# Queries and keys transposed by DMA instead of on TensorE, in a fused window attention and MoE kernel

## The chip, the cores and the metric

The kernel runs on one core of a Trainium2 chip. The time is device microseconds of that core; a kernel's time is the median of its runs. Ratios are computed as the mean time of one kernel's fast runs over that of the other's of the same rounds, so they are not quite the ratio of the medians quoted. In the profile PE is TensorE (PEld its weight loads), DVE is VectorE, ACT is ScalarE, POOL is GpSimd, and SP is the engine whose queue issues most DMAs. L198 is line 198 of the kernel that the sentence names.

## The reference

```python
# q, k, v: (8 batches, 8 heads, 576 tokens, 64)
scores = 0.125 * q @ k.T                       # per batch and head
scores = where(abs(i - j) <= 32, scores, -1e9) # a window of 65 keys
x      = softmax(scores) @ v                   # (4608 tokens, 512)
h      = x @ w_in                              # 512 -> 2048
out    = leaky_relu(h, 0.01) @ w_out           # 2048 -> 512
```

## The kernel before

Heads are taken in pairs (p and p + 4), so that 2 x 64 dimensions fill the 128 rows of a matmul (`128*128` in the trace). There are 64 attention steps: 8 batches x 2 halves of 288 tokens x 4 pairs. They are interleaved with MoE work, so that PE always has something to do. The parts that matter here:

```python
RUN = S // 96                        # 6 tokens = 1.5 KB per partition and head
def load_qk(b, p, behind=None):      # one DMA for q, one for k
    for into, src, name in ((qf, q, "qf"), (kf, k, "kf")):
        t = fload.tile([96, 2, RUN * D], FP32, name=f"{name}{p}")
        if behind is not None:       # a guard: a one-element DMA that waits for w_in
            nc.sync.dma_start(out=t[0:1, 0, 0:1], in_=behind.bitcast(FP32))
            behind = None
        nc.sync.dma_start(out=t, in_=src[b, p:H:NPAIR].rearrange("a (p c) d -> p a (c d)", c=RUN))
...
def transposes(b, first=False):      # six per tensor and pair, one group per yield
    ...
        for c in range(RUN):
            nc.tensor.transpose(tp[:, c], src[:, p, c].rearrange("p a d -> p (a d)"), ident[0:96, 0:96])
        tok = tp.rearrange("p c i -> p i c")        # back to token order, on ACT
        if which == "q":
            nc.scalar.activation(out=qT[b][:, p].rearrange("p (i c) -> p i c", c=RUN), in_=tok, func=AF.Copy)
        else:
            kT = attn.tile([128, S], BF16, name="kT")
            nc.scalar.activation(out=kT_v, in_=tok, func=AF.Copy)
            for a in range(2):                      # the key copies, into a block diagonal
                r = slice(64 * a, 64 * a + 64)
                nc.vector.tensor_copy(out=kbd[b % 2][r, p, :, r], in_=kT[r].rearrange("p (n j) -> p n j", j=64))
        yield
...
def weighted(i):                     # s: row sums, x: weighted values
    nc.tensor.matmul(s, ones_bd, pr[:, 0:HALF], start=True, stop=False, ...)
    nc.tensor.matmul(s[:, ...], ones_bd, pr[:, HALF:NCOL], start=False, stop=True, ...)
    ...                              # five matmuls into x
    nc.vector.reciprocal(r, s)
    nc.vector.tensor_mul(xT[:, p, t0:t0 + HALF], x, r)
```

The row sums `s` and the values `x` have one PSUM bank each, the matmul results `mm` three, the transposes one. In the steady part a batch's transposes come one group of six per step.

The softmax here doesn't subtract the row's maximum and nothing guards it: scores larger than these inputs give would overflow.

Of the kernel before, what the change touches and what calls it, by code (L numbers as in the profile page):

```python
# [16 lines left out]
def kernel(  # L17
# [11 lines left out]

    nc = tc.nc  # L30
# [23 lines left out]
    mmps = ctx.enter_context(tc.tile_pool(name="mmps", bufs=3, space=PS))  # L54
    scps = ctx.enter_context(tc.tile_pool(name="scps", bufs=1, space=PS))
    xps = ctx.enter_context(tc.tile_pool(name="xps", bufs=1, space=PS))
    tps = ctx.enter_context(tc.tile_pool(name="tps", bufs=1, space=PS))


    qf, kf, vf = {}, {}, {}  # L60
    RUN = S // 96

    def load_qk(b, p, behind=None):


        for into, src, name in ((qf, q, "qf"), (kf, k, "kf")):
            t = fload.tile([96, 2, RUN * D], FP32, name=f"{name}{p}")
            if behind is not None:
                nc.sync.dma_start(out=t[0:1, 0, 0:1], in_=behind.bitcast(FP32))
                behind = None  # L70
            nc.sync.dma_start(  # L71
                out=t, in_=src[b, p:H:NPAIR].rearrange("a (p c) d -> p a (c d)", c=RUN),
            )
            into[b, p] = t
# [33 lines left out]

    qb = const.tile([96, NPAIR, RUN, 2, D], BF16)
    kb = const.tile([96, NPAIR, RUN, 2, D], BF16)  # L110

# [5 lines left out]
    def clear(t, p):  # L117
# [12 lines left out]
        [(0, 0, 96), (2, 96, 128), (4, 224, 64), (1, 32, 128), (3, 160, 128)],  # L130
        [(4, 288, 64), (6, 352, 128), (8, 480, 96), (5, 288, 128), (7, 416, 128)],
    ]
    ODD = [32, 0]

    win = const.tile([128, 3, 128], BF16)
    nc.gpsimd.memset(win, 1.0)
    for lo in (0, 64):
# [3 lines left out]
            base=0, channel_multiplier=-1, pattern=[[0, 3], [1, 128]],  # L141
# [3 lines left out]
            base=2 * W, channel_multiplier=1, pattern=[[0, 3], [-1, 128]],  # L145
        )
    win_f = win.rearrange("p n c -> p (n c)")
    mask = [const.tile([128, NCOL], BF16, name=f"mask{i}") for i in range(2)]

    def make_masks():  # L150
        for hf in range(2):
            lo = W * (hf + 1)
            nc.gpsimd.tensor_copy(out=mask[hf][:, 0:HALF], in_=win_f[:, lo:lo + HALF])
            nc.gpsimd.tensor_copy(out=mask[hf][:, HALF:NCOL], in_=win_f[:, 0:NCOL - HALF])
# [8 lines left out]
    def cast_qk(b, p, q_eng=None):  # L163
        for eng, src, dst in ((q_eng or nc.gpsimd, qf, qb), (nc.gpsimd, kf, kb)):
            eng.tensor_copy(  # L165
                out=dst[:, p], in_=src[b, p].rearrange("p a (c d) -> p c a d", d=D),
            )
# [9 lines left out]
    def transposes(b, first=False):  # L177

        qT[b] = attn.tile([128, NPAIR, S], BF16, name="qT")
        for p in range(NPAIR):  # L180
            for which, src in (("q", qb), ("k", kb)):
                if first:
                    tp = mmps.tile([128, RUN, 96], BF16, name="tp0", tag="mm")
                else:
                    tp = tps.tile([128, RUN, 96], BF16, name="tp")
                for c in range(RUN):
                    nc.tensor.transpose(  # L187
                        tp[:, c],
                        src[:, p, c].rearrange("p a d -> p (a d)"),
                        ident[0:96, 0:96],  # L190
                    )

                tok = tp.rearrange("p c i -> p i c")
                if which == "q":
                    nc.scalar.activation(  # L195
                        out=qT[b][:, p].rearrange("p (i c) -> p i c", c=RUN), in_=tok, func=AF.Copy,
                    )
                else:  # L198
                    kT = attn.tile([128, S], BF16, name="kT")
                    kT_v = kT.rearrange("p (i c) -> p i c", c=RUN)  # L200
                    nc.scalar.activation(out=kT_v, in_=tok, func=AF.Copy)  # L201
# [272 lines left out]
```

## Time and profile before

The time before is 355.9 us in four runs, and 356.2 to 356.4 in later rounds.

| from the page of before | busy, share of 353.9 us | to be read as |
|---|---|---|
| PE | 324.3 us, 92% | the bound from 28 us on |
| DVE | 211.8 us, 60% | second; one reciprocal of 1.95 us per step |
| ACT | 183.4 us, 52% | has room |
| POOL | 178.7 us, 51% | has room |
| hardware DMA queue | 42.7% of 16 engines | share 0.9 to 1.3 until 53 us and 1.1 to 1.2 from 71 to 106, between and after these 0.1 to 0.6 |

A share of the whole span hides the stages, so the prediction starts from the table of windows.

### The profile page before, as it was taken

Reading aid. Unit: us, or ns where it says so; the run is one execution under the profiler, and the core shown is the slowest. Engines: PE = TensorE matmul, PEld = TensorE weight load, DVE = VectorE, ACT = ScalarE, POOL = GpSimd, SP = SyncE. Lnnn points to the kernel's source line nnn. Section 1 sums busy time; section 2 is a strip of 40 time slices with the busy share of each in tenths; the row PEclk is TensorE's granted clock in tenths of the full one; section 3 lists DMA queues with packets and bytes.
Section 4 is the critical chain, followed back from the end, with each engine's and each line's share of the span. In section 5 each row is a group of like instructions: output and inputs, shape, how many; then the busy total and the mean of one; then the engine's idle time right before and its main releaser. Section 6 shows DMA issues by size and latency. Waiting matters only on the chain.

```text
span 353.9 us, 6635 instructions
## 1 busy us (share of the span) xinstructions
PE 324.3 (92%) x2600; PEld 208.2 (59%) x2624; DVE 211.8 (60%) x242; ACT 183.4 (52%) x363; POOL 178.7 (51%) x213
## 2 busy tenths in 40 slices
PE   2658998999989898999999898999999999999995
PEld 1437864584957655656656555656656656555472
DVE  5588647757686877645653778554676676630101
ACT  5765862292845637518527527716528517326060
POOL 7797676578765766524543568533655423200000
PEclk9999999999999999999999999999999999999999
DMA  8999986599995274342453265340010010020101
GB/s 187 214 205 236 269 162 182 144 201 235 209 255 146 58 222 133 69 126 88 140 162 70 63 177 165 88 124 33 0 61 30 2 61 31 5 86 0 61 31 59
DMA packets 60707, 42.37 MB, mean 120 GB/s; under 512 B 39684, under 2 KB 56068, under 8 KB 60676
## 3 DMA queue, kind: packets, MB, share of 16 engines
q1 hardware_dynamic: 56388, 37.76, 42.7%
q0 software_dynamic: 4288, 4.20, 7.2%
q8 instruction: 20, 0.33, 0.4%
q14 instruction: 11, 0.09, 0.1%
HBM read 36.70 MB, written 9.44 MB: 130 GB/s over the span
## 4 chain that ended last, share of the span: by engine, by line
PE 77%; DMA 7%; DVE 6%; POOL 4%; SPq 2%; issue 2%; ACT 1%; DVEq 0%; POOLq 0%; ACTq 0%
PE mm L273 33%; PE mm L264 31%; DMA kf<-in_k_dram 7%; DVE r L252 5%; PE x L246 3%; PE tp L187 3%; PE ps L220 3%; PE s L238 2%; PE s L239 2%; SPq L71 1%; POOL vbd L175 1%; POOL vbd L400 1%; SPq L82 1%; DVE xT L254 1%; POOL pr L230 1%
## 5 line engine op out<-in xcount | busy, mean ns | idle before, releaser
L252 DVE RECIPROCAL r<-s 128x288 f32<-128x288 f32 x64 | 125.1, 1954 | 38.5 <-PE s L239 38.2
L230 POOL TENSOR_TENSOR pr<-e,mask 128x544 bf16<-128x544 bf16 x64 | 77.7, 1213 | 115.0 <-ACT e L226 114.7
L264 PE MATMUL mm<-xT,w_in_bf 128*128 128x384 bf16 (+1 forms) x896 | 132.7, 304 | 0.9 <-ACT kT L201 0.8
L268 ACT ACTIVATE gT<-mm 128x384 bf16<-128x384 f32 (+1 forms) x224 | 99.0, 445 | 63.0 <-PE mm L264 58.6
L273 PE MATMUL mm<-w_out_bf,gT 128*128 128x512 bf16 x552 | 126.8, 379 | 1.3
L264 PEld LDWEIGHTS <-w_in_bf 128*128 128x128 bf16 x896 | 86.6, 98 | 38.0 <-issue 1.3
L273 PEld LDWEIGHTS <-gT 128*128 128x128 bf16 x576 | 54.9, 98 | 61.1
L226 ACT ACTIVATE e<-ps 128x544 bf16<-128x544 f32 x64 | 39.8, 622 | 77.6 <-PE ps L220 77.6
L280 DVE COPY o_sb<-mm 128x512 f32<-128x512 f32 x36 | 24.9, 691 | 66.8 <-PE mm L273 66.8
L204 DVE COPY kbd<-kT 64x576 bf16<-64x576 bf16 x64 | 28.4, 444 | 18.2 <-ACT kT L201 17.6
L175 POOL CAST vbd<-vf 64x576 bf16<-64x576 f32 x58 | 38.3, 661 | 1.9
L254 DVE TENSOR_TENSOR xT<-x,r 128x288 bf16<-128x288 f32 x64 | 29.3, 458 | 7.0 <-PE mm L264 0.5
L165 POOL CAST kb<-kf 96x768 bf16<-96x768 f32 x32 | 26.6, 834 | 9.5 <-DMA kf<-in_k_dram 9.5
L246 PE MATMUL x<-pr,vbd 128*128 128x128 bf16 (+2 forms) x320 | 26.9, 217 | 2.0 <-POOL vbd L175 1.0
L220 PE MATMUL ps<-qT,kbd 128*128 128x128 bf16 (+2 forms) x320 | 27.3, 219 | 0.3
L238 PE MATMUL s<-pr,ones_bd 128*128 128x288 bf16 x64 | 19.0, 297 | 8.7 <-DVE r L252 7.0
L220 PEld LDWEIGHTS <-kbd 128*128 128x128 bf16 x320 | 21.1, 102 | 8.1 <-issue 0.6
L195 ACT ACTIVATE qT<-tp 128x576 bf16<-128x576 bf16 x32 | 20.8, 649 | 9.6 <-PE tp L187 9.0
L246 PEld LDWEIGHTS <-vbd 128*128 128x128 bf16 x320 | 21.4, 101 | 7.1 <-issue 2.8
L201 ACT ACTIVATE kT<-tp 128x576 bf16<-128x576 bf16 x32 | 20.8, 650 | 8.9 <-PE tp L187 7.9
L187 PE MATMUL tp<-ident,qb 96*128 96x96 bf16 x192 | 14.4, 214 | 8.5 <-DVE qb L165 6.7
L165 POOL CAST qb<-qf 96x768 bf16<-96x768 f32 x24 | 19.7, 820 | 0.0
(31 smaller groups left out, 107.7 us busy)
## 6 DMA issues: line engine op xcount, KB each, us to landing
qf<-in_q_dram SPq DMA_DIRECT2D x32, 288.0 KB, 3.5
kf<-in_k_dram SPq DMA_DIRECT2D x32, 288.0 KB, 3.9
vf<-in_v_dram SPq DMA_DIRECT2D x64, 144.0 KB, 3.4
out_dram<-o_sb SPq DMA_DIRECT2D x36, 256.0 KB, 2.2
w_in_bf<-in_moe_w_in_dram POOLq DMA_DIRECT2D x8, 256.0 KB, 6.4
w_out_bf<-in_moe_w_out_dram POOLq DMA_DIRECT2D x4, 512.0 KB, 13.5
qf<-w_in_bf SPq DMA_DIRECT2D x1, 0.0 KB
vf<-w_out_bf SPq DMA_DIRECT2D x1, 0.0 KB
```

What stands on the lines that cost most here:

```text
L165: eng.tensor_copy(out=dst[:, p], in_=src[b, p].rearrange("p a (c d) -> p c a d", d=D),)
L175: nc.gpsimd.tensor_copy(out=vbd[b % 2][r, p, :, r], in_=vf[b, p][r])
L204: nc.vector.tensor_copy(out=kbd[b % 2][r, p, :, r], in_=kT[r].rearrange("p (n j) -> p n j", j=64),)
L220: nc.tensor.matmul(ps[:, c0:c0 + n], kbd[b % 2][:, p, blk], qT[b][:, p, q0:q0 + n], start=True, stop=True,)
L226: nc.scalar.activation(out=e, in_=ps[:, 512 - HALF:512 - HALF + NCOL], func=AF.Exp, scale=scale,)
L230: nc.gpsimd.tensor_mul(pr, e, mask[hf])
L246: nc.tensor.matmul(x[:, a:a + n], vbd[b % 2][:, p, blk, :], pr[:, c0:c0 + n], start=(n_ == 0), stop=(n_ == len(WIN[hf]) - 1), skip_group_c ...
L252: nc.vector.reciprocal(r, s)
L254: nc.vector.tensor_mul(xT[:, p, t0:t0 + HALF], x, r)
L264: nc.tensor.matmul(h[:, 0:n], w_in_bf[:, c, ts(f, 128)], xT[:, c, ds(t0, n)], start=(c == 0), stop=(c == DMC - 1),)
L268: nc.scalar.activation(out=gT[t0][:, f, 0:n], in_=h[:, 0:n], func=AF.Prelu, alpha=0.01)
L273: nc.tensor.matmul(o, gT[t0][:, f, ts(j, 128)], w_out_bf[:, f, :], start=(f == 0), stop=(f == FFC - 1),)
```

## The change

The intent: take 288 transposes and the ACT copies behind them off the engines, and let the DMA engines, at a share of 0.1 to 0.6 after 106 us, do them. The DMA transposes of the diff leave the columns in the order of the tile they read (so the code is written). So the loads change to runs of four tokens (1 KB) over 48 partitions, queries keep the permuted order through scores, mask and row sums until the last product restores it, and keys are put back in order by the key copy.

```diff
+    qkf = [fload.tile([112, 2, NM, RUN * D], FP32, name=f"qkf{p}") for p in range(NPAIR)]   # RUN = 4, NM = 3
     def load_qk(b, p, behind=None):
-        for into, src, name in ((qf, q, "qf"), (kf, k, "kf")): ...      # one DMA each, 96 partitions
+        for r0, src in ((0, q), (key_row(b), k)):                       # two DMAs each, 48 partitions
             if behind is not None:
                 nc.sync.dma_start(out=rows[0:1, 0, 0, 0:1], in_=behind.bitcast(FP32))
-                behind = None
+            for a in range(2):
+                nc.sync.dma_start(out=rows[:, a],
+                    in_=src[b, NPAIR * a + p].rearrange("(m i c) d -> i m (c d)", i=NR, c=RUN))
...
+    def place_keys(b, p):                                               # the key copies
+            nc.vector.tensor_copy(
+                out=kbd[b % 2][r, p, :, r].rearrange("p n (i c) -> p n i c", c=RUN),
+                in_=t[r].rearrange("p (c n i) -> p n i c", c=RUN, n=NB))
+    def transpose_pe(b, p): ...                                         # batches 0 and 1
+    def transpose_dma(b, p):                                            # batches 2 to 7
+        for r0, t in ((0, qT[b][:, p]), (key_row(b), kT[b, p])):
+            nc.sync.dma_start_transpose(out=t.rearrange("p (g i) -> p g i", i=NR),
+                in_=qkb[r0:r0 + NR, p].rearrange("p c m a d -> p (c m a d)"))
...
+    for b in range(2, B):
+        for p in range(NPAIR):
+            i = 8 * (b - 1) + p + (3 if b == 2 else 0)
+            plan(i + 3, place_keys, b, p)
+            plan(i + 1, transpose_dma, b, p)
+            plan(i, cast_qk, b, p)
+            ...                                                         # and the next loads
```

Cut from it: the masks in the new order, the row sums in five matmuls with the windows of `x` instead of two, one cast for q and k together (halved between DVE and POOL in batches 0 and 1), and a fourth matmul bank in place of the transpose bank.

More of the change, by code (lines that the diff above doesn't have):

```diff
@@ L53, with key_row @@
     PS = bass.MemoryType.PSUM
-    mmps = ctx.enter_context(tc.tile_pool(name="mmps", bufs=3, space=PS))
+    mmps = ctx.enter_context(tc.tile_pool(name="mmps", bufs=4, space=PS))
     scps = ctx.enter_context(tc.tile_pool(name="scps", bufs=1, space=PS))
     xps = ctx.enter_context(tc.tile_pool(name="xps", bufs=1, space=PS))
-    tps = ctx.enter_context(tc.tile_pool(name="tps", bufs=1, space=PS))
-    qf, kf, vf = {}, {}, {}
-    RUN = S // 96
+    vf = {}
+    RUN = 4
+    NI = S // RUN
+    NR = 48
+    NM = NI // NR
+    qkf = [fload.tile([112, 2, NM, RUN * D], FP32, name=f"qkf{p}") for p in range(NPAIR)]
+    def key_row(b):
+        return NR if b < 2 else 64
     def load_qk(b, p, behind=None):
-        for into, src, name in ((qf, q, "qf"), (kf, k, "kf")):
-            t = fload.tile([96, 2, RUN * D], FP32, name=f"{name}{p}")
+        for r0, src in ((0, q), (key_row(b), k)):
+            rows = qkf[p][r0:r0 + NR]
             if behind is not None:
-                nc.sync.dma_start(out=t[0:1, 0, 0:1], in_=behind.bitcast(FP32))
-                behind = None
-            nc.sync.dma_start(
-                out=t, in_=src[b, p:H:NPAIR].rearrange("a (p c) d -> p a (c d)", c=RUN),
-            )
-            into[b, p] = t
+                nc.sync.dma_start(out=rows[0:1, 0, 0, 0:1], in_=behind.bitcast(FP32))
+            for a in range(2):
+                nc.sync.dma_start(
+                    out=rows[:, a],
+                    in_=src[b, NPAIR * a + p].rearrange("(m i c) d -> i m (c d)", i=NR, c=RUN),
+                )
     def load_v(b, p, behind=None):
@@ L106 @@
     nc.vector.memset(ones_bd[64:128, 64:128], 1.0)
-    qb = const.tile([96, NPAIR, RUN, 2, D], BF16)
-    kb = const.tile([96, NPAIR, RUN, 2, D], BF16)
+    qkb = const.tile([112, NPAIR, RUN, NM, 2, D], BF16)
     kbd = [const.tile([128, NPAIR, NB, 128], BF16, name=f"kbd{i}") for i in range(2)]
@@ L129 @@
     WIN = [
-        [(0, 0, 96), (2, 96, 128), (4, 224, 64), (1, 32, 128), (3, 160, 128)],
-        [(4, 288, 64), (6, 352, 128), (8, 480, 96), (5, 288, 128), (7, 416, 128)],
-    ]
-    ODD = [32, 0]
-    win = const.tile([128, 3, 128], BF16)
+        [(0, 0, 24), (2, 24, 32), (4, 56, 16), (1, 8, 32), (3, 40, 32)],
+        [(4, 72, 16), (6, 88, 32), (8, 120, 24), (5, 72, 32), (7, 104, 32)],
+    ]
+    win = const.tile([128, RUN, 32], BF16)
     nc.gpsimd.memset(win, 1.0)
@@ L140 @@
             out=w, in_=w, compare_op=ALU.is_ge, fill=0.0,
-            base=0, channel_multiplier=-1, pattern=[[0, 3], [1, 128]],
+            base=0, channel_multiplier=-1, pattern=[[1, RUN], [RUN, 32]],
         )
@@ L144, with make_mask @@
             out=w, in_=w, compare_op=ALU.is_ge, fill=0.0,
-            base=2 * W, channel_multiplier=1, pattern=[[0, 3], [-1, 128]],
+            base=2 * W, channel_multiplier=1, pattern=[[-1, RUN], [-RUN, 32]],
         )
-    win_f = win.rearrange("p n c -> p (n c)")
     mask = [const.tile([128, NCOL], BF16, name=f"mask{i}") for i in range(2)]
-    def make_masks():
-        for hf in range(2):
-            lo = W * (hf + 1)
-            nc.gpsimd.tensor_copy(out=mask[hf][:, 0:HALF], in_=win_f[:, lo:lo + HALF])
-            nc.gpsimd.tensor_copy(out=mask[hf][:, HALF:NCOL], in_=win_f[:, 0:NCOL - HALF])
+    def make_mask(hf):
+        c0 = 0
+        for blk, q0, n in WIN[hf]:
+            lo = q0 - 16 * blk + 8
+            nc.gpsimd.tensor_copy(
+                out=mask[hf][:, c0:c0 + RUN * n].rearrange("p (c i) -> p c i", c=RUN),
+                in_=win[:, :, lo:lo + n],
+            )
+            c0 += RUN * n
     xT = const.tile([128, NPAIR, NTOK], BF16)
@@ L161, with cast_qk @@
     qT = {}
-    def cast_qk(b, p, q_eng=None):
-        for eng, src, dst in ((q_eng or nc.gpsimd, qf, qb), (nc.gpsimd, kf, kb)):
-            eng.tensor_copy(
-                out=dst[:, p], in_=src[b, p].rearrange("p a (c d) -> p c a d", d=D),
-            )
+    def cast_qk(b, p):
+        rows = slice(0, key_row(b) + NR)
+        src = qkf[p][rows].rearrange("p a m (c d) -> p c m a d", d=D)
+        parts = ((nc.vector, 0, 2), (nc.gpsimd, 2, 4)) if b < 2 else ((nc.gpsimd, 0, 4),)
+        for eng, c0, c1 in parts:
+            eng.tensor_copy(out=qkb[rows, p, c0:c1], in_=src[:, c0:c1])
     def cast_v(b, p, on_act=False):
@@ L175, in cast_v @@
                 nc.gpsimd.tensor_copy(out=vbd[b % 2][r, p, :, r], in_=vf[b, p][r])
-    def transposes(b, first=False):
-        qT[b] = attn.tile([128, NPAIR, S], BF16, name="qT")
-        for p in range(NPAIR):
-            for which, src in (("q", qb), ("k", kb)):
-                if first:
-                    tp = mmps.tile([128, RUN, 96], BF16, name="tp0", tag="mm")
-                else:
-                    tp = tps.tile([128, RUN, 96], BF16, name="tp")
-                for c in range(RUN):
-                    nc.tensor.transpose(
-                        tp[:, c],
-                        src[:, p, c].rearrange("p a d -> p (a d)"),
-                        ident[0:96, 0:96],
-                    )
-                tok = tp.rearrange("p c i -> p i c")
-                if which == "q":
-                    nc.scalar.activation(
-                        out=qT[b][:, p].rearrange("p (i c) -> p i c", c=RUN), in_=tok, func=AF.Copy,
-                    )
-                else:
-                    kT = attn.tile([128, S], BF16, name="kT")
-                    kT_v = kT.rearrange("p (i c) -> p i c", c=RUN)
-                    nc.scalar.activation(out=kT_v, in_=tok, func=AF.Copy)
-                    for a in range(2):
-                        r = slice(64 * a, 64 * a + 64)
-                        nc.vector.tensor_copy(
-                            out=kbd[b % 2][r, p, :, r],
-                            in_=kT[r].rearrange("p (n j) -> p n j", j=64),
-                        )
-                yield
@@ new lines, with new_T @@
+    kT = {}
+    def new_T(b, p):
+        if p == 0:
+            qT[b] = attn.tile([128, NPAIR, S], BF16, name="qT")
+        kT[b, p] = attn.tile([128, S], BF16, name="kT", bufs=3)
+    def place_keys(b, p):
+        t = kT.pop((b, p))
+        for a in range(2):
+            r = slice(64 * a, 64 * a + 64)
+            nc.vector.tensor_copy(
+                out=kbd[b % 2][r, p, :, r].rearrange("p n (i c) -> p n i c", c=RUN),
+                in_=t[r].rearrange("p (c n i) -> p n i c", c=RUN, n=NB),
+            )
@@ new lines, in transpose_pe @@
+    def transpose_pe(b, p):
+        new_T(b, p)
+        for h in range(2):
+            tp = mmps.tile([128, 2 * NM, 2, NR], BF16, name="tp", tag="mm")
+            for g in range(2 * NM):
+                nc.tensor.transpose(
+                    tp[:, g].rearrange("p w i -> p (w i)"),
+                    qkb[0:2 * NR, p, 2 * h + g // NM, g % NM].rearrange("p a d -> p (a d)"),
+                    ident[0:2 * NR, 0:2 * NR],
+                )
+            half = slice(h * S // 2, (h + 1) * S // 2)
+            for w, t in enumerate((qT[b][:, p], kT[b, p])):
+                nc.scalar.activation(
+                    out=t[:, half].rearrange("p (g i) -> p g i", i=NR),
+                    in_=tp[:, :, w], func=AF.Copy,
+                )
+        place_keys(b, p)
@@ L210 @@
+    def transpose_dma(b, p):
+        new_T(b, p)
+        for r0, t in ((0, qT[b][:, p]), (key_row(b), kT[b, p])):
+            nc.sync.dma_start_transpose(
+                out=t.rearrange("p (g i) -> p g i", i=NR),
+                in_=qkb[r0:r0 + NR, p].rearrange("p c m a d -> p (c m a d)"),
+            )
     probs = {}
@@ L218, in score @@
         c0 = 512 - HALF
+        qv = qT[b][:, p].rearrange("p (c i) -> p c i", c=RUN)
         for blk, q0, n in WIN[hf]:
             nc.tensor.matmul(
-                ps[:, c0:c0 + n], kbd[b % 2][:, p, blk],
-                qT[b][:, p, q0:q0 + n], start=True, stop=True,
+                ps[:, c0:c0 + RUN * n].rearrange("p (c i) -> p c i", c=RUN),
+                kbd[b % 2][:, p, blk], qv[:, :, q0:q0 + n], start=True, stop=True,
             )
-            c0 += n
+            c0 += RUN * n
         e = attn.tile([128, NCOL], BF16, name="e")
@@ L235, in weighted @@
         pr = probs.pop(i)
-        x = xps.tile([128, HALF], FP32, name="x")
-        s = xps.tile([128, HALF], FP32, name="s")
-        nc.tensor.matmul(s, ones_bd, pr[:, 0:HALF], start=True, stop=False, skip_group_check=True)
-        nc.tensor.matmul(
-            s[:, ODD[hf]:ODD[hf] + NCOL - HALF], ones_bd, pr[:, HALF:NCOL],
-            start=False, stop=True, skip_group_check=True,
-        )
-        c0 = 0
-        for n_, (blk, q0, n) in enumerate(WIN[hf]):
-            a = q0 - HALF * hf
-            nc.tensor.matmul(
-                x[:, a:a + n], vbd[b % 2][:, p, blk, :], pr[:, c0:c0 + n],
-                start=(n_ == 0), stop=(n_ == len(WIN[hf]) - 1), skip_group_check=True,
-            )
-            c0 += n
-        r = attn.tile([128, HALF], FP32, name="r")
-        nc.vector.reciprocal(r, s)
-        t0 = b * S + hf * HALF
-        nc.vector.tensor_mul(xT[:, p, t0:t0 + HALF], x, r)
+        x = xps.tile([128, RUN, HALF // RUN], FP32, name="x")
+        s = xps.tile([128, RUN, HALF // RUN], FP32, name="s")
+        for out_, weights in ((s, lambda blk: ones_bd), (x, lambda blk: vbd[b % 2][:, p, blk, :])):
+            c0 = 0
+            for n_, (blk, q0, n) in enumerate(WIN[hf]):
+                i0 = q0 - HALF // RUN * hf
+                nc.tensor.matmul(
+                    out_[:, :, i0:i0 + n], weights(blk),
+                    pr[:, c0:c0 + RUN * n].rearrange("p (c i) -> p c i", c=RUN),
+                    start=(n_ == 0), stop=(n_ == len(WIN[hf]) - 1), skip_group_check=True,
+                )
+                c0 += RUN * n
+        r = attn.tile([128, HALF // RUN, RUN], FP32, name="r")
+        nc.vector.reciprocal(r, s.rearrange("p c i -> p i c"))
+        t0 = b * S + hf * HALF
+        nc.vector.tensor_mul(
+            xT[:, p, t0:t0 + HALF].rearrange("p (i c) -> p i c", c=RUN),
+            x.rearrange("p c i -> p i c"), r,
+        )
     gT = {}
@@ L284, with plan @@
     NC = 2 * NPAIR * B
-    state = {"tp": 8, "done": 0}
-    t_parts = {}
-    PLAN = (
-        ((0, 0, 0, 0, 0, 2, 4, 6), ((), (), (), (), (0,), (1, 2), (3,), ()),
-         ((), (), (), (), (), (), (0,), (1, 2, 3))),
-        ((0, 1, 2, 3, 4, 5, 6, 7), ((0,), (1,), (2,), (3,), (), (), (), ()),
-         ((), (), (), (), (0,), (1,), (2,), (3,))),
-    )
-    def step_transposes(upto):
-        while state["tp"] < min(upto, 8 * B):
-            b = state["tp"] // 8
-            if b not in t_parts:
-                t_parts[b] = transposes(b)
-            next(t_parts[b])
-            state["tp"] += 1
+    state = {"done": 0}
+    todo = {}
+    def plan(i, f, *args):
+        todo.setdefault(i, []).append((f, args))
+    for b in range(2, B):
+        for p in range(NPAIR):
+            i = 8 * (b - 1) + p + (3 if b == 2 else 0)
+            j = (14, 15, 15, 15)[p] if b == 2 else 8 * (b - 1) + 4 + p
+            plan(i + 3, place_keys, b, p)
+            plan(i + 1, transpose_dma, b, p)
+            plan(i, cast_qk, b, p)
+            plan(j, cast_v, b, p)
+            if b + 1 < B:
+                plan(i, load_qk, b + 1, p)
+                plan(j, load_v, b + 1, p)
+    first_of = (place_keys, transpose_dma, cast_qk, cast_v, load_qk, load_v)
     def step():
         i = state["done"]
-        b, r = i // 8, i % 8
-        if b > 0:
-            upto = 8 * (b + 1) + PLAN[b > 1][0][r]
-            step_transposes(max(upto - 1, 8 * (b + 1)))
         if i + 1 < NC and i != 7:
@@ L316, in step @@
         weighted(i)
-        if b > 0:
-            step_transposes(upto)
-        if 0 < b < B - 1:
-            for p in PLAN[b > 1][1][r]:
-                cast_qk(b + 1, p)
-                if b + 2 < B:
-                    load_qk(b + 2, p)
-            for p in PLAN[b > 1][2][r]:
-                cast_v(b + 1, p)
-                if b + 2 < B:
-                    load_v(b + 2, p)
         state["done"] += 1
+        for f, args in sorted(todo.pop(i, []), key=lambda t: first_of.index(t[0])):
+            f(*args)
     w_in_r = moe_w_in.rearrange("(a u d) f -> a d u f", a=2, d=D)
@@ L342, in load_w_out @@
         nc.gpsimd.dma_start(out=w_out_bf[:, c, :], in_=w_out_r[:, c, :])
-    first = transposes(0, first=True)
-    def first_pair():
-        next(first)
-        next(first)
-    cast_qk(0, 0, nc.vector)
-    make_masks()
-    cast_qk(0, 1, nc.vector)
-    first_pair()
-    first_pair()
+    cast_qk(0, 0)
+    make_mask(0)
+    cast_qk(0, 1)
+    transpose_pe(0, 0)
+    transpose_pe(0, 1)
     clear(vbd[0], 2)
     cast_v(0, 0)
-    cast_qk(0, 2, nc.vector)
+    cast_qk(0, 2)
     score(0)
     load_w_in(0, 512)
-    first_pair()
+    transpose_pe(0, 2)
     clear(vbd[0], 3)
-    cast_qk(0, 3, nc.vector)
+    cast_qk(0, 3)
     load_w_in(512, 1024)
@@ L373 @@
         if i == 0:
-            first_pair()
+            transpose_pe(0, 3)
+            make_mask(1)
     state["done"] = NPAIR
@@ L390 @@
     for p in range(NPAIR):
-        cast_qk(1, p, nc.vector)
+        cast_qk(1, p)
     for p in range(NPAIR):
         load_v(1, p, w_out_bf[0:1, 4, 0:2] if p == 0 else None)
-    second = transposes(1, first=True)
     for f in range(FFC):
@@ L397 @@
         if f % 4 == 3:
-            next(second)
-            next(second)
+            transpose_pe(1, f // 4)
             nc.gpsimd.memset(vbd[1][:, f // 4], 0.0)
-    state["tp"] = 16
     score(8)
```

## The prediction

> **What bounds the kernel now.** I read the table of windows first, because PE's busy share of the whole span (92%) mixes a loading phase with a steady one.
>
> ```profile
> 20.00:30.00 10.00, 6.73 (x49) 4.55 (x48) 9.12 (x7) 3.92 (x7) 9.47 (x11) 1.00 1.24 205
> ...
> 120.00:140.00 20.00, 18.17 (x156) 11.26 (x157) 16.66 (x20) 9.83 (x19) 15.07 (x18) 1.00 0.59 162
> 140.00:160.00 20.00, 19.89 (x144) 11.52 (x144) 10.35 (x12) 8.66 (x17) 7.82 (x10) 1.00 0.36 94
> ```
>
> The columns are stretch, length, busy time of PE, PEld, DVE, ACT and POOL, granted clock, DMA share, GB/s. Until about 28 us PE starves while the DMA engines are full. From 140 us on it is busy 19.9 of 20 us at full clock, and the DMA engines are at 0.4 or below, except in 120 to 140 and 200 to 220 us, where DVE is busy nearly 17 of 20 us.
>
> Next, the list of waits, for PE alone and from 60 us to the end:
>
> ```profile
> PE s L238 <- DVE r L252: 3.8, 5, 1.2
> PE tp L187 <- ACT qT L195: 2.2, 3, 0.7
> PE x L246 <- DVE xT L254: 0.8, 5, 0.2
> PE x L246 <- POOL vbd L175: 0.6, 1, 0.6
> PE s L238 <- POOL pr L230: 0.4, 1, 0.4
> ```
>
> 7.8 us of waiting in 294 us: work taken from PE there shortens the span, unless it lay beside one of these waits. The chain of waits in order of time (start, length) shows one attention step among the MoE matmuls:
>
> ```profile
> 165.65 0.24 PE ps L220 x5
> 165.89 0.12 PE s L238
> 166.01 0.11 PE s L239
> 166.12 0.32 PE x L246 x5
> 166.44 0.26 PE tp L187 x6
> 166.70 3.90 PE mm L264 x24
> ```
>
> Six transposes (half of one head pair's query or key) are 0.26 us on the path. The third view is the groups by form, for what stands beside PE:
>
> ```profile
> L252 DVE RECIPROCAL r<-s 128x288 f32<-128x288 f32 x64 | 125.1, 1954 | 38.5 <-PE s L239 38.2
> ...
> L254 DVE TENSOR_TENSOR xT<-x,r 128x288 bf16<-128x288 f32 x64 | 29.3, 458 | 7.0 <-PE mm L264 0.5
> L204 DVE COPY kbd<-kT 64x576 bf16<-64x576 bf16 x64 | 28.4, 444 | 18.2 <-ACT kT L201 17.6
> L165 POOL CAST kb<-kf 96x768 bf16<-96x768 f32 x32 | 26.6, 834 | 9.5 <-DMA kf<-in_k_dram 9.5
> ...
> L201 ACT ACTIVATE kT<-tp 128x576 bf16<-128x576 bf16 x32 | 20.8, 650 | 8.9 <-PE tp L187 7.9 <-PE mm L264 0.7
> ```
>
> DVE is the second engine: 1.95 + 0.46 us per step, and two key copies of 0.44 us per pair, that is, per two steps.
>
> [...](1) [...] One new transpose is 48 rows by 1536 bf16, 147 KB[...]. The trace of before has no such DMA. (2) [...]the new copy reads every 144th element. (3) [...] The trace speaks against a large cost on reads: ACT reads the transposes with a stride (L201) and takes 650 ns for 576 elements, against 490 for 384 contiguous ones in L268, 0.83 ns an element.
>
> **The change, part by part.**
>
> *Transposes off PE, batches 2 to 7.* 6 batches x 4 pairs x 2 tensors = 48 groups of six, by 0.255 us: 12.2 us less on PE, all after 60 us. Not all counts. In the five places where PE waits for the reciprocal, two steps run with no MoE between, and a group of transposes stood inside that wait; 5 x 0.26 = 1.3 us stay as idle. Net 10.9 us. Of the 2.2 us in which PE waited for ACT to empty the one transpose bank, I count 1.5 as gained (one of the three lay in such a double step). ACT loses 48 x 0.65 = 31 us, but it is busy 52% of the span and sets no end: 0. The fourth matmul bank: no wait for one is listed, 0.
>
> *Row sums in five matmuls instead of two.* The same 544 columns. The five of x or ps take 0.24 us where the two of s take 0.23: 56 steps by under 0.01 us, +0.4 us. Moving operands now come in four runs of 16 to 32 columns; I assume full rate.
>
> *Key copies.* [...]they now fall in four steps running per batch (the fourth to the seventh) instead of every second one. [...] PE's period: steps run from about 74 to 305 us, 231/51 = 4.5 us, some 4.3 after the saving. DVE comes level with PE for four steps and catches up in the next four. The row-sum bank is single, so a backlog of over some 1.7 us shows as a stall; I allow 0.3 us per batch, +2 us. Reciprocal and product read PSUM with a stride: by (3), 0.
>
> *Casts.* One of 1536 elements for two of 768 on POOL: even.
>
> *Loads.* Runs of 1 KB for 1.5 KB. From 320 to 340 us only outputs move: share 0.11 x 16 engines x 20 us = 35 us for 41 GB/s x 20 us = 400 runs of 2 KB, 88 ns each. The hardware queue's total is 42.7% x 16 x 353.9 = 2418 us for 4608 such runs, 36864 of 256 B (v) and 12288 of 1536 B (q, k). A cost of a + b x bytes fits these with a = 23 ns and b = 0.032 ns: 72 ns for a run of 1536 B, 55 for 1024 (an estimate). A pair's load goes from 384 x 72 = 27.6 to 576 x 55 = 31.7 us of engine time, +0.26 us on 16 engines; eight pairs in the first two batches, +2 us in the phase where DMA is full. The key load of batch 1 also gets a second one-element guard DMA, whose like was waited for 3.8 us by the issuing queue; other loads fill the engines meanwhile. PE's waits from 30 to 60 us are only 2 us, so the last keys of batch 1, which land at 46.7 us, come just in time, and a delay passes on: +2 us.
>
> *DMA transposes.* 48 of 147 KB from about 70 us on. Each has two steps (8 us) before the key copy that needs it, and DVE[...] would wait if it were late. Between two and five us each I count 0.
>
> Sum: 356.2 - 10.9 - 1.5 + 0.4 + 2.0 + 2.0 = 348.2. I put 348.
>
> **The rivals.**
> *The DMA transposes are slow.* [...] In milder form (3 us, beside loads that keep the engines at 0.8 to 1.1 between 60 and 100 us) DVE waits in a key copy, the reciprocals behind it slip and PE stalls: 352 to 362. [...] Against it: the share of 0.4 and less after 140 us, and a plan that gives two steps of room.
> *DVE becomes the bound.* If the strided copy costs 1.2 us, or the product slows on strided PSUM (+0.3 us x 64), four steps per batch take 5.2 us against 4.3: some 3 us per batch, 355 to 360. For it: the two stretches near 17 of 20. Against: 38 us of idle before the reciprocals.
> *The start eats it.* If the first two batches land 5 us later: 351, "same".
> *The good case.* [...]the start is even: 356.2 - 12.4 + 0.4 = 344.
>
> **Range and chances.** The gain of 12 us is counted from the path and is safe as a debit; what is unsure is what comes back. The good case is 344, my sum 348, the mild rivals 351 to 360; the range is 341 to 360. Faster by over 2% means under 349.1, just above my value, so 0.55; within 2% 0.32; slower, the slow transposes and little else, 0.13.
>
> **What would show it.** Right: no L187-like groups on PE after 60 us, PE busy 19.9 of 20 in most windows, the steady part 8 to 12 us shorter; [...]DMA transposes landing within 5 us; the end of the first 60 us 1 to 3 us later. Wrong: key copies waiting for a DMA, waits of PE for the reciprocal well above 5 us, five-matmul groups longer than 0.25 us, or a DMA share near 1 after 140 us.

## The result, and the profile after

The changed kernel takes 384.2 us (383.8 to 385.2) against 355.9 us: a ratio of 1.079, with an interval of 1.075 to 1.083. It is 28 us slower; 348 had been predicted. The table of windows, with the columns named in the prediction, first two lines of the kernel before and then the changed kernel:

```profile
80.00:100.00 20.00, 19.13 (x182) 14.02 (x183) 13.92 (x17) 11.92 (x26) 15.33 (x20) 1.00 1.13 230
100.00:120.00 20.00, 17.78 (x178) 13.35 (x178) 14.70 (x18) 11.81 (x26) 11.86 (x15) 1.00 0.64 157
```

```profile
60.00:80.00 20.00, 18.44 (x162) 11.77 (x162) 17.23 (x17) 5.97 (x13) 13.79 (x15) 1.00 0.67 138
80.00:100.00 20.00, 10.33 (x91) 7.32 (x90) 8.82 (x8) 5.00 (x12) 7.28 (x7) 0.80 1.27 175
100.00:120.00 20.00, 15.83 (x134) 10.94 (x134) 15.65 (x15) 8.02 (x19) 11.48 (x13) 0.95 1.24 188
120.00:140.00 20.00, 14.98 (x140) 10.67 (x139) 15.91 (x16) 7.38 (x17) 10.83 (x12) 1.00 1.20 171
140.00:160.00 20.00, 14.52 (x105) 8.19 (x104) 13.35 (x13) 3.60 (x8) 8.01 (x8) 0.83 1.05 144
```

PE, which before was busy 17.8 to 19.9 of 20 us in these stretches, is down to 10 to 16 from 80 to 160 us. The DMA share there is 1.05 to 1.27, where it had been 1.13 from 80 to 100 us and 0.36 to 0.64 after that, and yet the engines move no more than 190 GB/s. The granted clock, 1.00 throughout before, falls to 0.80 and 0.83.

Where the time is lost can be placed with the reciprocals, one per step in both kernels. The changed kernel's k-th starts later than that of before by 6.3 us at step 4, 9.7 at step 8, 6.1 at step 14, 15.6 at step 15, 25.8 at step 24, 31.8 at step 31 and 29.8 at step 63. So some 6 to 10 us are lost in the start and 25 between steps 14 and 31; after that 2 come back.

What PE waits for from 60 us on, in the list of waits of the changed kernel (engine, line, releaser, us, times, longest):

```profile
PE ps L240 <- DVE kbd L198: 13.7, 3, 9.6
PE s L262 <- DVE r L269: 12.8, 12, 4.7
PE s L262 <- POOL vbd L185: 2.3, 1, 2.3
PE ps L240 <- ACT e L246: 1.3, 4, 0.4
```

The waits for transposes are gone, as planned. In their place stand 13.7 us for the key copy and 12.8 instead of 3.8 us for the reciprocal, both on DVE. The groups say what became of the key copy and of the cast:

```profile
L198 DVE COPY kbd<-kT 64x576 bf16<-64x576 bf16 x64 | 72.2, 1128 | 16.8 <-DMA kT<-qkb 14.1 <-ACT kT L215 2.1
...
L177 POOL CAST qkb<-qkf 112x1536 bf16<-112x1536 f32 x24 | 35.1, 1463 | 3.4 <-DMA qkf<-in_k_dram 3.4
```

A key copy takes 1128 ns, not the 444 of before, and DVE is idle 14.1 us ahead of these copies because a DMA transpose has not landed. The longest such case can be followed in the timelines. On the issuing queue (start, duration, instruction, count):

```profile
82.40 7.75 SPq L90 DMA_DIRECT2D vf<-in_v_dram  x8
90.25 1.49 SPq L224 DMA_TRANSPOSE qT<-qkb  x1
91.84 1.36 SPq L224 DMA_TRANSPOSE kT<-qkb  x1
```

On DVE and then on PE:

```profile
86.59 0.46 DVE L271 TENSOR_TENSOR xT<-x,r 128x288 bf16<-128x288 f32 x1
95.51 2.24 DVE L198 COPY kbd<-kT 64x576 bf16<-64x576 bf16 x2 [8.46 <-DMA kT<-qkb]
```

```profile
84.57 3.62 PE L293 MATMUL mm<-w_out_bf,gT 128*128 128x512 bf16 x15
97.81 0.64 PE L240 MATMUL ps<-qT,kbd 128*128 128x96 bf16 x5 [9.62 <-DVE kbd L198]
...
99.14 5.13 PE L293 MATMUL mm<-w_out_bf,gT 128*128 128x512 bf16 x16
```

The first cast of batch 2 was done at 75.1 us. Its transposes are issued only at 90.25 and 91.84 us: ahead of them in the queue stand loads of q and k until 82 us, and then eight loads of v, which take 7.75 us to issue while the DMA engines are full (a share of 1.4 from 87 us on). DVE runs nothing else meanwhile and waits 8.5 us; PE waits 9.6 us for DVE. When PE starts again it runs slowly: five score matmuls need 0.64 us, not 0.40. The windows of one microsecond show a granted clock of 0.50 from 92 to 102 us: in this trace it falls 3.8 us after PE's last matmul and is back at 1.00 some 4.3 us after PE restarts. If the clock is taken as either 1.00 or 0.50, the mean of 0.971 makes 0.029 / 0.5 x 383.5 = 22 us at 0.50, in part idle (an estimate).

The DMA engines' own account, before and then after:

```profile
q1 hardware_dynamic: 56388, 37.76, 42.7%
```

```profile
q1 hardware_dynamic: 92742, 44.85, 68.2%
...
qT<-qkb SPq DMA_TRANSPOSE x24, 4.8
kT<-qkb SPq DMA_TRANSPOSE x24, 4.5
```

The columns of the queue are packets, MB and the share of 16 engines' span; those of the transposes, count and median us from issue to landing. 68.2% of 16 x 383.5 us is 4185 us of engine time, against 2418 before.

### The profile page after: what moved, and what is told of

The parts are those of the page before. It is cut to its first block, busy times and chain, and to the rows that moved or that the text cites. A ratio compares the mean times of both kernels' runs of the same rounds, so it can differ in the third digit from the quotient of the medians.

```text
span 383.5 us, 6561 instructions
## 1 busy us (share of the span) xinstructions
PE 321.7 (84%) x2505; PEld 202.3 (53%) x2528; DVE 257.9 (67%) x242; ACT 155.2 (40%) x331; POOL 177.9 (46%) x195
## 3 DMA queue, kind: packets, MB, share of 16 engines
q1 hardware_dynamic: 92742, 44.85, 68.2%
## 4 chain that ended last, share of the span: by engine, by line
PE 48%; DVE 20%; DMA 15%; SPq 7%; POOL 4%; issue 4%; ACT 1%; DVEq 0%; POOLq 0%; ACTq 0%
PE mm L293 24%; PE mm L284 18%; DMA qkf<-in_k_dram 10%; DVE r L269 9%; DVE kbd L198 8%; SPq L79 3%; DMA kT<-qkb 3%; SPq L90 2%; PE x L262 2%; PE ps L240 2%; PE s L262 2%; POOL qkb L177 2%; DVE xT L271 2%; DMA qkf<-w_in_bf 1%; POOL pr L250 1%
## 5 line engine op out<-in xcount | busy, mean ns | idle before, releaser
L293 PE MATMUL mm<-w_out_bf,gT 128*128 128x512 bf16 x553 | 132.6, 390 | 1.5 <-issue 0.4
L293 PEld LDWEIGHTS <-gT 128*128 128x128 bf16 x576 | 56.8, 101 | 65.2 <-issue 7.4
L198 DVE COPY kbd<-kT 64x576 bf16<-64x576 bf16 x64 | 72.2, 1128 | 16.8 <-DMA kT<-qkb 14.1
L177 POOL CAST qkb<-qkf 112x1536 bf16<-112x1536 f32 (+1 forms) x32 | 44.6, 1394 | 14.2 <-DMA qkf<-in_k_dram 12.8
L262 PE MATMUL s<-pr,ones_bd 128*128 128x128 bf16 (+2 forms) x320 | 27.6, 220 | 19.1 <-DVE r L269 16.3
L262 PEld LDWEIGHTS <-ones_bd 128*128 128x128 bf16 x320 | 18.3, 102 | 23.1 <-DVE r L269 22.9
L262 PEld LDWEIGHTS <-vbd 128*128 128x128 bf16 x320 | 20.2, 102 | 6.0 <-issue 4.5
L208 PE MATMUL tp<-ident,qkb 96*128 96x96 bf16 x96 | 7.8, 242 | 15.2 <-DVE qkb L177 15.0
L208 PEld LDWEIGHTS <-qkb 96*128 96x128 bf16 x96 | 6.1, 117 | 16.7 <-DVE qkb L177 15.7
L177 DVE CAST qkb<-qkf 96x768 bf16<-96x768 f32 x8 | 8.2, 1023 | 8.6 <-DMA qkf<-in_k_dram 8.5
```

The costliest lines, as they stand in the source:

```text
L177: eng.tensor_copy(out=qkb[rows, p, c0:c1], in_=src[:, c0:c1])
L198: nc.vector.tensor_copy(out=kbd[b % 2][r, p, :, r].rearrange("p n (i c) -> p n i c", c=RUN), in_=t[r].rearrange("p (c n i) -> p n i c", c= ...
L262: nc.tensor.matmul(out_[:, :, i0:i0 + n], weights(blk), pr[:, c0:c0 + RUN * n].rearrange("p (c i) -> p c i", c=RUN), start=(n_ == 0), stop ...
L293: nc.tensor.matmul(o, gT[t0][:, f, ts(j, 128)], w_out_bf[:, f, :], start=(f == 0), stop=(f == FFC - 1),)
```

## The experiments

**The plan.** After the traces four causes were to be told apart: the DMA transposes (engine time and place in the queue), the key copies, the second guard, and the loads in 1 KB runs with what follows them. They were undone in turn, first from the changed kernel and then on top of each other, so that the steps add up. Then the idea was tried on the kernel before. In five of the experiments (those on the changed kernel with key copies in runs of 16, except the last benchmark) the result is wrong on purpose, with keys or tokens in wrong places, yet each passed the comparison. The scores explain it: a product of 64 terms of 0.1 x 0.1, by 0.125, has a spread of about 0.01, so the weights are nearly equal, and the order of tokens within a window hardly changes the sum. The comparison is therefore weak on order, for the two kernels and for the variants alike.

### Transposes of all batches on PE

```diff
-            plan(i + 1, transpose_dma, b, p)
+            plan(i + 1, transpose_pe, b, p)      # key copies stay at i + 3; keys in rows 48 to 95
```

> The changed kernel with the transposes of batches 2 to 7 put back on PE (12 per pair, in the new layout), all else as changed. If the load of the DMA engines by the DMA transposes is the larger cause (steps 14 to 25 lose 19 us there): 24 to 28 us less from the middle, 12 us more of PE work, so about 368 us. If the slow key copies (1128 ns) are the larger cause and the middle stays DVE-bound: 384 us or more, since PE work is only added. DMA share of 80 to 180 us falls from about 1.2 to 0.6 in either case.

Measured: 375.8 us, 8.4 less than the changed kernel, although PE has 288 transposes more. Step 15 starts 7.7 us behind the kernel before instead of 15.6, so the long wait at the turn is gone. PE still waits 10.0 us for the reciprocal, and the end was 8 us worse than that theory's number. Both theories of the expectation were too simple: there are two causes of like size, as the next two runs show. The DMA share of 80 to 180 us fell from 1.18 to 0.71 in the mean, less far than the 0.6 expected. The hardware queue:

```profile
q1 hardware_dynamic: 63558, 37.76, 44.9%
```

That is 44.9% of 16 x 374.7 = 2692 us of engine time, so a DMA transpose cost (4185 - 2692) / 48 = 31 us, or 1.9 us of all 16 engines. A batch has eight of them: 15.5 us. This is a difference of totals: what the transposes added to the time of the loads beside them is in it.

### Key copies in runs of 16

```diff
-                out=kbd[b % 2][r, p, :, r].rearrange("p n (i c) -> p n i c", c=RUN),
-                in_=t[r].rearrange("p (c n i) -> p n i c", c=RUN, n=NB),
+                out=kbd[b % 2][r, p, :, r].rearrange("p n (c i) -> p n c i", c=RUN),
+                in_=t[r].rearrange("p (c n i) -> p n c i", c=RUN, n=NB),
```

> The changed kernel with the key copy reading and writing runs of 16 contiguous elements (keys in another order within a block, so a wrong result on purpose). Copy 1128 to about 450 ns. If DMA load is the larger cause: 372 to 376 us (4 us at the start, some 3 us per batch in the three DVE-bound batches at the end, the middle unchanged). If the key copies are the larger cause: 358 us or less.

Measured: 378.7 us, 5.5 less, short of both numbers. The median copy falls to 328 ns, but the longest takes 3923 ns, and DVE now waits 22.4 us for DMA transposes ahead of the copies instead of 14.1. In the middle, time that DVE had spent copying it now spends waiting: there the DMA was the wall behind the copies. The packed copy is not the copy of the kernel before either: that one took 433 to 451 ns in all 64 cases, the packed one 306 ns at best but 620 in the mean here and 667 in the next run, since some took longer, up to those 3923 ns. So the 5.5 us are the gain from this other copy.

### Both edits

> Both edits at once (wrong result on purpose). What is left is the start (1 KB loads, second guard, casts that wait for both tensors) and the row sums in five matmuls. If these two causes are the whole loss but for the start: 356 to 360 us. If something else in the new layout costs (strided moving operands, row sums), above 364 us.

Measured: 370.3 us, 14 above the kernel before. The two causes together are worth 13.9 us, the sum of 8.4 and 5.5. The first number (356 to 360) fails. The second (above 364) holds, but not for the reason given with it, row sums and strided operands: most of the rest lies in the start, where step 8 is 11 us behind. The timelines of this run show, on DVE and on POOL, what became of the last key copies of batch 1:

```profile
53.76 8.17 DVE L198 COPY kbd<-kT 64x576 bf16<-64x576 bf16 x8
```

```profile
54.46 4.19 POOL L402 MEMSET vbd<- 128x1152 bf16 x4
```

Eight copies of about 0.3 us take 8.2 us, and one of them 3.9, while POOL runs four memsets. The copy of 3.9 us, from 53.76 to 57.70, spans the end of a cast and three memsets of POOL. Whether POOL held it up was not shown; the second benchmark below did not show a copy of that length again.

### Single operations after the last output

The changed kernel with single operations on otherwise idle engines behind it; each DMA waits for the one before.

> The changed kernel, and after its last output single operations one at a time on idle engines: DMA transposes of 48x1536, a 288 KB query load in 1.5 KB runs and in 1 KB runs, a 144 KB load in 256 B runs, and the key copy in both forms on DVE, ACT and POOL. If the transposes are slow in themselves: 4 us or more each alone; if they were only behind loads: 2 to 2.5 us alone. The loads in 1 KB runs: 10 to 15% longer than in 1.5 KB runs. Key copy strided 1128 ns on DVE alone too (if it was contention with POOL, under 800); on ACT 650 to 700 in either form.

Measured (one look): a DMA transpose in 7.35 / 3 = 2.45 us; a 288 KB query load in 6.59 / 3 = 2.20 us in runs of 1.5 KB and 7.84 / 3 = 2.61 us in runs of 1 KB, 19% longer and so above the 10 to 15% expected. The key copy with its strided source took 0.64 us on DVE, 1.17 on ACT and 1.13 on POOL, against 0.45, 0.68 and 0.66 from runs of 16. The 0.64 seemed to speak for contention in the kernel. But here the destination was without gaps and of one half of the partitions, so the control differed in more than the surroundings, and was repeated below.

### One guard instead of two

```diff
                 nc.sync.dma_start(out=rows[0:1, 0, 0, 0:1], in_=behind.bitcast(FP32))
+                behind = None
```

The reason, on the issuing queue of the changed kernel:

```profile
28.88 0.80 SPq L79 DMA_DIRECT2D qkf<-in_q_dram  x2
29.73 0.62 SPq L77 DMA_DIRECT2D qkf<-w_in_bf  x1
35.10 0.80 SPq L79 DMA_DIRECT2D qkf<-in_k_dram  x2
```

> The changed kernel with one guard DMA before the loads of batch 1, as before, instead of two. The second guard held the issuing queue from 29.7 to 35.1 us. If that wait delays batch 1: step 8 (63.7 us) 4 to 5 us earlier and the time 380 us. If the loads were limited by the DMA engines anyway: step 8 and the time unchanged within 1 us.

Measured: 381.9 us, 2.3 less; step 8 comes 1.3 us earlier, not 4 to 5. In the 5.4 us of the second guard the DMA engines had other work: their share there was 1.17 in the changed kernel.

### Three edits: PE transposes, packed copies, one guard

> PE transposes, packed key copies (keys of a block in another order, values not: a wrong result on purpose, though the comparison may not see it) and one guard: 370.3 less 5 = 365 us if the guard counts, 370 if not. What is left above 356 is then the 1 KB loads, the casts that wait for both tensors, and the transposes in blocks of twelve.

Measured: 368.8 us, 1.5 less than without the guard edit, but step 8 is still 11.5 us behind. The gain isn't where the guard stands, and the run without the edit spreads from 369.0 to 371.0 us, so these 1.5 us are not shown to be the guard's.

### DMA transposes in some batches only

```diff
-            plan(i + 1, transpose_dma, b, p)
+            plan(i + 1, transpose_pe if b < 5 else transpose_dma, b, p)   # or b < 3
```

> The changed kernel with the transposes of batches 2 to 4 on PE and of 5 to 7 by DMA, where fewer loads run beside them. If DMA transposes hurt only beside loads: the 375.8 us of all on PE less 24 groups of 0.26 = 6 us, about 370. If they hurt wherever they are (key copies that wait, queue order): 376 us or more.

> The changed kernel with the transposes of batch 2 alone on PE and of batches 3 to 7 by DMA. From batch 5 on by DMA gave 371.4 us, all by DMA 384.2, none 375.8. If the loss is made at the turn from start to steady part, where batch 2's transposes queue behind the loads of v: 371 to 373 us. If it is made by every batch whose transposes run beside loads: 377 us or more.

Measured: 371.4 us from batch 5 on and 375.0 us from batch 3 on. With none (375.8) and all (384.2) this makes a series: the three last batches by DMA gain 4.4 us, batches 3 and 4 lose 3.5, batch 2 loses 9.2. The run from batch 5 on spreads from 367.9 to 372.6 us, so the first two steps of this series are rough. They fit the first expectation's theory (transposes hurt only beside loads). The second one's numbers both fail: the turn at batch 2 is the largest loss, but not the only one.

### Loads in 1.5 KB runs again

On top of the three edits, q and k are loaded by one DMA each, over 96 partitions, as before.

> PE transposes, packed copies and one guard as in the run with all three, and the loads of q and k again one DMA each over 96 partitions in runs of 1.5 KB, into the same tile (tokens in wrong places: a wrong result on purpose, though the comparison may not see it). If the 1 KB runs and the doubled number of DMAs cost the start: step 8 from 11.5 us behind the kernel before to 6 or less, and 362 to 364 us. If the start is lost in casts and key copies after the loads have landed: step 8 stays 10 or more behind and the time within 2 us of 368.8.

Measured: 361.5 us, 7.3 less, and step 8 only 3.1 us behind, not 11.5. So it was the loads: their form (run length, partitions and number of DMAs were changed together, so which of the three counts is not shown) is worth 7.3 us, gained in the start, against 2 us predicted for the run length.

### Transposes of a pair in two halves

On top of that, from batch 3 on the twelve transposes of a pair come as two groups of six in successive steps, and the key copies in every second step.

> The run with 1.5 KB loads (361.5 us), with the twelve transposes of a pair split into two groups of six in successive steps from batch 3 on, and the key copies spread over every second step, as before. If the blocks of twelve in the double steps (three times some 2.7 us[...]) are most of the 5 us left: 357.5 to 359 us. If the row sums in five matmuls or the strided operands are: 361 us, unchanged.

Measured: 358.3 us, a ratio of 1.008 (1.002 to 1.014) to the kernel before, so all but 2 us are accounted for. The mean clock is 0.998 or 0.999 in three of the four runs; in the experiment before, the four runs had 0.991 to 1.000, and the one at 1.000 took 359.2 us. The spreads overlap (357.5 to 362.6 here, 359.2 to 362.9 there), so the gain of 3.3 us is less sure than the others. What is left, row sums in five matmuls among it, is 2 us or less.

### Single operations again

> The changed kernel, and after its last output the key copy with its true destination: alone, strided and packed, then both beside memsets on POOL; then eight DMA transposes to four destinations, four loads of 147 KB, and loads and transposes in turn. If the strided copy is slow by its form: 1.1 us alone and the same beside POOL. If it was slow by contention: 0.65 alone. Packed: 0.31 alone, and up to 4 us beside the memsets if DVE has to wait for POOL. Transposes in a row without other traffic: one per 1.3 us if the issuing queue sets their rate, 2 us or more if the DMA engines do; in turn with loads 4 us or more per pair.

Measured (one look), on DVE, on POOL and on the issuing queue:

```profile
378.41 1.11 DVE L453 COPY kbd<-kT 64x576 bf16<-64x576 bf16 x1
```

```profile
381.45 4.05 POOL L461 MEMSET vbd<- 128x1152 bf16 x4
```

```profile
378.52 10.95 SPq L472 DMA_TRANSPOSE qT<-qkb  x8
```

The strided copy into its true place takes 1.11 us alone and 1.13 beside the memsets: it is slow by its form. The packed copy takes 0.32 to 0.34 us alone, and two of the four beside memsets took 1.13, about the length of one memset; the 3.9 us of the run with both edits did not come again, and why that copy took so long stays open. Eight transposes in a row go out one per 1.37 us, with the engines at a share of about 0.7: 0.7 x 16 x 1.37 = 15 us of engine time each. That is half of the 31 us that one cost beside loads in the changed kernel. The pace is near the 1.3 us expected if the issuing queue sets it, and the engines are not full. In turn with loads a load and a transpose took 2.6 to 3.2 us per pair, not the 4 or more expected.

### The idea on the kernel before

The loads, the token order and the key copies stay as before. From batch 3 on the six transposes of a tensor become one DMA transpose of the same 96-partition tile into a staging tile, issued one or more steps after the cast and used two or more steps later; ACT's reordering copy reads the staging tile. To make room, `gT` is 384 columns wide instead of 512, of which only 384 were used.

```diff
+    def issue_T(b, p):
+        for which, src in (("q", qb), ("k", kb)):
+            t = attn.tile([128, RUN, 96], BF16, name="tT", bufs=6)
+            nc.sync.dma_start_transpose(out=t, in_=src[:, p].rearrange("p c a d -> p (c a d)"))
+            tT[b, p, which] = t
```

> The kernel before, its loads, layout and packed key copies untouched, with the transposes of batches 3 to 7 by DMA from the same 1.5 KB tiles into a staging tile, and ACT doing the reordering copy from there (1.2 us instead of 0.65). PE loses 40 groups of 0.26 = 10 us. If the idea is sound and only its layout and its place were wrong: 347 to 351 us, faster than both. If DMA transposes beside loads cost what they save: 355 us or more.

> The kernel before with late DMA transposes (351.2 us) and the transpose bank given to the matmuls (four instead of three). PE waited 2.6 us for ACT to empty a bank there. If a fourth bank covers these: 348.5 to 349.5 us; if the waits come from ACT being behind for longer than a bank lasts: 351.

> The same with the query's reordering copy on POOL instead of ACT. If ACT's added 1.18 us copies are what PE waits for: 347.5 to 349 us. If POOL's copy delays the masking product[...]: slower than the four-bank run, 350 us or more.

Measured: 351.2 us (ratio 0.986, interval 0.981 to 0.991), then 348.5 us with the transpose bank given to the matmuls (0.979, 0.975 to 0.984), then 347.3 us with the query's reordering copy on POOL (0.975, 0.970 to 0.980). All three beat both kernels, though only the last is faster by 2% beyond the noise. Its runs fall in two pairs, 345.6 and 346.0 at a mean clock of 1.000, 348.6 and 349.2 at 0.988. The step from ACT to POOL is smaller than that spread, so it is not shown. What PE waits for there from 60 us on, and when the transposes land:

```profile
PE s L263 <- DVE r L277: 5.7, 5, 1.2
PE ps L245 <- ACT e L251: 1.7, 5, 0.4
PE x L271 <- DVE xT L279: 0.8, 5, 0.2
PE x L271 <- POOL vbd L174: 0.6, 1, 0.6
PE s L263 <- POOL pr L255: 0.4, 1, 0.4
```

```profile
tT<-qb SPq DMA_TRANSPOSE x20, 3.1
tT<-kb SPq DMA_TRANSPOSE x20, 3.2
```

PE waits 9.2 us and nowhere for a transpose; they land in 3.1 us. Step 63 starts 9.9 us before that of the kernel before: the 40 groups of 0.26 us are 10.4 us. With the DMA transposes alone only half of that arrived, 5.1 us; there PE waited 2.6 us for ACT to empty a matmul bank, and the fourth bank brought 2.7 us more. The fourth bank on the kernel before, without DMA transposes, was not tried; PE waited there only 2.2 us for the transpose bank and for no matmul bank from 60 us on, which bounds what it could bring. These three keep the layout of the kernel before; that their order is right rests on the code, the comparison being weak there.

## Why the prediction was wrong

Undone one after the other, the parts lead from the changed kernel back to the one before:

| undone | us | gain |
|---|---|---|
| nothing | 384.2 | |
| DMA transposes | 375.8 | 8.4 |
| and strided key copies | 370.3 | 5.5 |
| and the second guard | 368.8 | 1.5 |
| and the loads in 1 KB runs | 361.5 | 7.3 |
| and the blocks of twelve transposes | 358.3 | 3.3 |
| the kernel before | 356.3 | 2.0 |

**Transposes off PE (a gain of 10.9, and 1.5 of waits).** Right in mechanism: no transpose on PE after 60 us, no wait of PE for one. For the size the late-transpose kernels speak: of the 10 us counted for their 40 groups they got 5.1 with the DMA transposes alone, 7.8 with the fourth bank, which the changed kernel has too, and 9.0 at last. In the changed kernel the gain was buried.

**DMA transposes ("Between two and five us each I count 0").** This is the step that failed; the estimate rested on no trace, that of before having no such DMA. They did land in that time, 4.8 and 4.5 us in the median. But a median from issue to landing leaves out the wait to be issued, and the cost to everything else. One transpose took 31 us of engine time, and DVE and PE waited for the late ones: the first two were issued 15 us after their cast, and DVE was idle 14.1 us ahead of the key copies. Since undoing them gained 8.4 us and put some 11 us of PE work back on the path, their gross cost was about 19 us, an estimate from these two numbers. The rival "in milder form", a wait of DVE in the key copy with the reciprocals behind it slipping, is what happened. Its 352 to 362 us were too small (348 and 19 are 367), and it named neither the clock of 0.50 nor the queue; how much each of these is worth was not measured.

**Key copies (+2).** Mechanism right, size off: the 2 us, with DVE drawing level with PE, rested on the estimate of the new copy's time, which no trace had shown; the copy took 1128 ns after 444. A step with two of them is 1.95 + 0.46 + 2 x 1.13 + 0.1 = 4.8 us, before any output copy, against PE's 4.3: DVE sets the pace in those steps instead of drawing level. In the trace the reciprocals from 163 to 177 us start 4.7 to 4.8 us apart. The rival "DVE becomes the bound" had named this cost (1.2 us). Worth 5.5 us in place of 2.

**Loads and guard (+4).** Mechanism right, size off: 7.3 us for the loads in place of 2, and 1.5 to 2.3 for the guard against 2, though not seen at step 8 in the second of its two tests. Engine time per run was a fair account of the engines (19% longer alone, 15% predicted), but at step 8 these few per cent had become 8 us. That the start depends on when the last of several loads lands is argued, not shown. This was the rival "The start eats it".

**The range.** All three rivals came about in the same run, the transposes for some 19 us (the estimate above), the start for 7 and the key copies for 5.5. The range to 360 us took them one at a time.

**Casts (even).** Even on POOL in the steady part (1463 ns for two of about 825). In the first batches DVE's casts rose from a mean of 707 to 1023 ns. That both engines then cast at the same time does not explain it: they do so in the run with both edits too, where the mean is 678. What it costs was not measured.

**Row sums (+0.4).** Not contradicted: 0.24 us for five matmuls, and at most 2 us left for all that was not undone.

**The blocks of twelve** were not in the prediction. They do not exist in the changed kernel after batch 1, only in the experiments on the way back; so those 3.3 us belong to the way of undoing, and the DMA transposes' own net cost is, against transposes in groups of six, nearer to 12 us than to 8, an estimate from the two steps.

Still open: why the same bytes take twice the engine time beside loads, and how much of the loss is engine time and how much the place in the queue. The series of batches gives a hint: with the form unchanged, the 24 transposes of the last three batches cost (56.0% of 16 x 366.1 = 3280, less 2692) / 24 = 25 us each, the 24 of batches 2 to 4, beside more loads, (4185 - 3280) / 24 = 38. This speaks for crowding. The transposes of 96 rows in the late-transpose kernel took (54.9% of 16 x 349.6 = 3071, less 2418) / 40 = 16 us each although some loads ran beside them; what the rows and the loads' form add was not separated.

## What to carry to other kernels

Work moved to an idle resource is free only where it is idle at that time: the DMA share of the stage (here 1.05 to 1.27 from 80 to 160 us), the place in the issuing queue (here 15 us from the first cast to the issue) and the engine time per operation (here 31 us) must be counted as for any engine, and a median landing time (here 4.8 and 4.5 us) shows none of them. A change of layout should be priced at its worst access pattern (here the key copy, 1128 ns after 444). When a change has one sound idea and several companions, the idea alone on the old kernel, in the stage that has room, is the experiment to make first: here it turned 28 us of loss into 5 of gain by itself, and 9 with the matmul bank that it set free and a copy moved to POOL.
